# Reordering a decode kernel's loop: key transposes one quarter step ahead, VectorE's small steps one behind, values spread over four quarters, constants ahead of the query projection

## The chip, the cores and the metric

The kernel runs on one core of a Trainium2 chip. The metric is the device time of one execution, in microseconds (us). Profiled times are within the span of the core; a timed run is 1.7 to 1.8 us longer than its span (212.74 against 211.0 for the changed kernel, 224.66 against 222.9 for the profiled run of the kernel before). Each timed run comes with its granted TensorE clock and with a state: on one core, a run over 1.5% above the fastest run of the same kernel in the same set counts as slow and is left out of ratios.

## The reference, cut to what matters

One token for each of four sequences goes through an attention block and an MLP block in parallel. Attention reads a window of 2048 keys and values for 16 heads from the cache; that is nearly all of the data.

```python
# B=4, D=576, 32 query heads, 16 kv heads, 128 per head, window W=2048, F=4608
xn = _layernorm(x)
q = xn @ wq                                   # wq: 4.7 MB
scores = einsum(q, k_window) * Dh**-0.5       # k, v: 2 x 16 heads x 2 MB
o = softmax(scores) @ v_window
A = o @ wo                                    # wo: 4.7 MB
x1 = xn + gather(gelu(layernorm(xn) @ w1)) @ w2   # [the four shifts give zeros for one token]
B = x1 + gelu(layernorm(x1) @ w3) @ w4        # w3, w4: 5.3 MB each
return x + A + B
```

With one token every shifted group of `h` is padding, so the kernel never reads w1 and w2.

## The kernel before: the parts that the change touches

The loop has one step t for each head and four quarter steps s. Head t's scores, head t-1's softmax, head t-2's values and head t-3's output share a step. K arrives with positions on partitions, so VectorE transposes each quarter (`kt`) before TensorE can multiply it with the queries (`qz`). In the timelines below, the matmuls of TensorE and the instructions of VectorE each follow the order of the program, so an instruction that waits holds up those behind it. These names recur in the profiles: `kn` and `vn` are K and V tiles; `mx` is the maximum of a head's scores; `mg` is those maxima gathered by TensorE, which VectorE reduces to `nm`; `dn` is the denominator of the softmax, which VectorE inverts to `rd`; `oT` is the head's transposed output, which VectorE sums into `on`; `acc` collects the final sums.

```python
kvp = tile_pool(name="kv", bufs=6)                      # six K or V tiles of 2 MB
ktp = tile_pool(name="kt", bufs=3)
...
def k_transpose(h, s):                                  # VectorE
    kt = ktp.tile([P, 2, SC, QD], I32, tag="kt")
    nc.vector.transpose(out=kt[:], in_=src)             # quarter s of K
def k_scores(h, s):                                     # TensorE: 4 matmuls 128x512
    ...
def sm_maxT(h):
    nc.tensor.matmul(out=mg[:], lhsT=sel_jb[:], rhs=dm) # TensorE ...
    nc.vector.reduce_max(out=nm[:], in_=mg[:], ...)     # ... and VectorE at once behind it
def o_turn(h):
    ...                                                 # 4 TensorE transposes of O_sb to oT
    nc.vector.reduce_sum(out=on..., in_=oT...)          # VectorE at once behind them
# [sm_den + reciprocal, o_spread + mk and op: the same pattern]

for t in range(Hkv):
    hm, hv, hf = t - 1, t - 2, t - 3
    for s in range(NSL):
        k_transpose(t, s)
        if s == 0:
            sm_max(hm); o_turn(hf); k_mask(t)
        k_scores(t, s)
        if s == 0:   sm_maxT(hm)
        elif s == 1: sm_sub(hm); sm_exp(hm); o_spread(hf)   # o_spread, o_proj: every 4th head
        elif s == 2: o_proj(hf)
        elif s == 3: sm_turn(hm); sm_den(hm); pv(hv); o_scale(hv)
        # [t == 7: the MLP's first product and its gelu]
    # [free K tile t and V tile t-2; issue the next loads]
```

The loads go out in one order: wq, K0, K1, K2, then V(h) and K(h+3) in turn, with a wo tile ahead of V0, V4, V8 and V12, w3 between V2 and K5, and w4 last. A K or V load waits for one of the six tiles to come free.

## Time and profile before

| | kernel before |
|---|---|
| time, median of 3 (range) | 229.6 us (226.83 to 230.71) |
| span of the profiled run | 222.9 us |
| data read | 87.17 MB |
| DMA engines busy | all the time, from 5 to about 206 us |
| last scores | about 201.5 us |
| from there to the end | about 21 us |

The page of the kernel before, cut into 40 slices of 5.6 us. The digits of PE and DVE (TensorE and VectorE) are busy tenths, PEclk is the granted TensorE clock in tenths, DMA the busy share of the DMA engines:

```profile
span 222.9 us, 2388 instructions
PE   0046139759696876589763968678758756876893
DVE  4952889685667876642257568454877766374120
PEclk9999555995969999979995599958999996699589
DMA  6999999999999999999999999999999999999000
GB/s 239 429 441 435 432 421 441 425 426 429 426 420 436 444 412 435 438 435 426 429 429 426 438 426 426 435 432 432 400 405 439 438 426 429 418 431 399 16 0 2
```

The DMA row is full until slice 37, then three slices are empty while TensorE still works. Neither compute engine is full anywhere in the loop.

The costliest groups of the kernel before. After the count come busy time and mean ns, then the engine's idle time just before these instructions and what ended it:

```profile
L328 PE MATMUL S<-kt,qz 128*128 128x512 bf16 x256 | 79.6, 449 | 33.4 <-DVE kt L203 33.4
L203 DVE STREAM_TRANSPOSE kt<-kn 128x1024 int32<-128x1024 int32 x64 | 76.1, 1217 | 0.6 <-PE S L328 0.3
```

VectorE's own waits for TensorE's small results, from the list of waits (total us, times, longest):

```profile
DVE rd L365 <- PE dn L363: 23.2, 15, 4.2
DVE nm L343 <- PE mg L341: 15.5, 15, 1.1
DVE on L391 <- PE oT L385: 12.1, 14, 4.1
```

TensorE stood idle for 33.4 us waiting for transposed keys, while VectorE, which makes them, never waited for a K load (`kn`). One ordinary step of the kernel before, from the timeline (start, duration, engine, instruction, idle time before):

```profile
154.81 1.07 PE L328 MATMUL S<-kt,qz 128*128 128x512 bf16 x4
155.81 0.17 PE L341 MATMUL mg<-dm,sel_jb 128*8 128x16 bf16 x1
156.02 0.17 DVE L343 TENSOR_REDUCE nm<-mg 8x1 bf16<-8x16 f32 x1 [1.13 <-PE mg L341]
156.11 3.47 DVE L203 STREAM_TRANSPOSE kt<-kn 128x1024 int32<-128x1024 int32 x3
157.38 1.06 PE L328 MATMUL S<-kt,qz 128*128 128x512 bf16 x4 [1.40 <-DVE kt L203]
```

Here is the ping-pong: VectorE idles 1.13 us for `mg`, which stands on TensorE behind four score matmuls; the next three transposes stand on VectorE behind that wait; and TensorE then idles 1.40 us for the first of them.

The chain that ended last in the kernel before begins at 206 us, after the stream, and has no DMA in it (its longest pieces; start, duration, what):

```profile
205.97 2.25 issue
...
211.89 1.97 PE acc L307 x16
...
215.19 4.36 PE acc L307 x68
```

### The profile page before, as it was taken

To read this page: it belongs to the slowest core of one execution; us is meant where nothing else is said; L and a number is where in the kernel's file an instruction comes from. 1 tells how busy PE (TensorE), PEld (TensorE's weight loads), DVE (VectorE), ACT (ScalarE), POOL (GpSimd) and SP (SyncE) were. 2 spreads that over 40 slices of the span, in tenths; PEclk is the share of its full clock that TensorE was granted. 3 is DMA by queue.
4 is the path that set the end of the run, shared out by engine and by line. 5 is a ranking of instruction groups with operands and counts; after the bars stand their busy time and mean duration, and the time that the engine had idled before them with its cause. 6 is when DMAs were issued, how large, how long until landed. Compare 5 with 4: busy or idle time off the path is not lost. (4 is left out here: it accounts for less than half of the span.)

```text
span 222.9 us, 2388 instructions
## 1 busy us (share of the span) xinstructions
PE 148.8 (67%) x955; PEld 63.0 (28%) x955; DVE 134.1 (60%) x230; ACT 26.5 (12%) x56; POOL 13.7 (6%) x20
## 2 busy tenths in 40 slices
PE   0046139759696876589763968678758756876893
PEld 0022013222332323143331323223323321333362
DVE  4952889685667876642257568454877766374120
ACT  2001000001111211112120112101112111112110
POOL 6940030000000000000000000000000000000000
PEclk9999555995969999979995599958999996699589
DMA  6999999999999999999999999999999999999000
GB/s 239 429 441 435 432 421 441 425 426 429 426 420 436 444 412 435 438 435 426 429 429 426 438 426 426 435 432 432 400 405 439 438 426 429 418 431 399 16 0 2
DMA packets 6797, 87.32 MB, mean 392 GB/s; under 512 B 758, under 2 KB 770, under 8 KB 1282
## 3 DMA queue, kind: packets, MB, share of 16 engines
q1 hardware_dynamic: 6778, 87.17, 92.1%
q8 instruction: 7, 0.11, 0.2%
q14 instruction: 4, 0.03, 0.0%
q10 hardware_dynamic: 8, 0.00, 0.0%
HBM read 87.17 MB, written 0.00 MB: 391 GB/s over the span
## 5 line engine op out<-in xcount | busy, mean ns | idle before, releaser
L328 PE MATMUL S<-kt,qz 128*128 128x512 bf16 x256 | 79.6, 449 | 33.4 <-DVE kt L203 33.4
L203 DVE STREAM_TRANSPOSE kt<-kn 128x1024 int32<-128x1024 int32 x64 | 76.1, 1217 | 0.6 <-PE S L328 0.3
L328 PEld LDWEIGHTS <-qz 128*128 128x128 bf16 x256 | 24.7, 105 | 69.9 <-issue 56.3
L353 ACT ACTIVATE E<-S 128x512 bf16<-128x512 f32 x16 | 9.6, 597 | 97.9 <-PE S L347 97.9
L385 PE MATMUL oT<-ident_w,O_sb 128*128 128x128 f32 x64 | 11.0, 296 | 12.0 <-ACT O_sb L379 12.0
L374 PE MATMUL O<-vn,PT 128*32 128x512 bf16 x256 | 18.4, 411 | 0.0
L379 ACT ACTIVATE O_sb<-O,rd 128x512 f32<-128x512 f32 x16 | 11.0, 687 | 61.3 <-issue 43.4
L365 DVE RECIPROCAL rd<-dn 128x1 f32<-128x1 f32 x16 | 2.7, 166 | 23.2 <-PE dn L363 23.2
L359 DVE STREAM_TRANSPOSE PT<-E 128x512 bf16<-128x512 bf16 x16 | 11.2, 701 | 3.1 <-ACT E L353 3.1
L385 PEld LDWEIGHTS oT<-ident_w,O_sb 128*128 128x128 f32 x64 | 7.0, 145 | 19.7 <-ACT O_sb L379 19.5
L343 DVE TENSOR_REDUCE nm<-mg 8x1 bf16<-8x16 f32 x16 | 2.6, 164 | 15.5 <-PE mg L341 15.5
L391 DVE TENSOR_REDUCE on<-oT 128x8 bf16<-128x128 f32 x16 | 4.7, 291 | 12.1 <-PE oT L385 12.1
L334 DVE TENSOR_REDUCE mx<-S 128x1 f32<-128x512 f32 x16 | 10.5, 656 | 1.4 <-PE S L328 1.4
L188 PE MATMUL tp<-ident_bf,first 4*128 4x4 bf16 x8 | 0.6, 172 | 13.1 <-DVE first L175 13.1
L175 DVE TENSOR_SCALAR first<-first,mv,rstd 4x576 bf16<-4x576 bf16 x2 | 8.1, 4074 | 1.4 <-POOL rstd L174 1.4
L363 PEld LDWEIGHTS dn<-rs,same_j 128*128 128x128 f32 x32 | 6.7, 213 | 5.0 <-ACT E L353 1.5
L307 PE MATMUL acc<-wo_sb,op 128*32 128x288 bf16 x64 | 7.5, 405 | 0.0
L244 POOL MEMSET qz<- 128x8216 bf16 x1 | 6.9, 6934 | 0.0
L374 PEld LDWEIGHTS <-PT 128*32 128x32 bf16 x256 | 5.6, 99 | 4.6 <-issue 1.3
L347 PE MATMUL S<-nm,j_row 8*128 8x512 bf16 x16 | 6.6, 412 | 0.3 <-DVE nm L343 0.3
L319 PE MATMUL S<-negbig,ohT 4*128 4x512 bf16 x16 | 6.4, 398 | 0.0
L307 PE MATMUL acc<-w_sb,gT 128*32 128x288 bf16 x72 | 5.7, 316 | 0.0
(88 smaller groups left out, 82.5 us busy)
## 6 DMA issues: line engine op xcount, KB each, us to landing
kn<-in_A_k_cache_dram SPq DMA_DIRECT2D x16, 2048.0 KB, 18.6
vn<-in_A_v_cache_dram SPq DMA_DIRECT2D x16, 2048.0 KB, 16.0
wo_sb<-in_A_wo_dram SPq DMA_DIRECT2D x4, 1152.0 KB, 18.8
w_sb<-in_B_w_dram SPq DMA_DIRECT2D x2, 2304.0 KB, 19.1
wq_sb<-in_A_wq_dram SPq DMA_DIRECT2D x2, 2048.0 KB, 9.5
w_sb<-in_B_w_dram SPq DMA_DIRECT2D x2, 1440.0 KB, 21.3
w_sb<-in_B_w_dram SPq DMA_DIRECT2D x3, 576.0 KB, 24.7
w_sb<-in_B_w_dram SPq DMA_DIRECT2D x1, 1152.0 KB, 20.9
```

Source lines behind the costliest of these rows:

```text
L175: nc.vector.tensor_scalar(out=dst_bf[:], in0=src[:], scalar1=mv[:, 0:1], scalar2=rstd[:, 0:1], op0=ALU.subtract, op1=ALU.mult)
L203: nc.vector.transpose(out=kt[:], in_=src)
L244: nc.gpsimd.memset(qz[:], 0.0)
L307: nc.tensor.matmul(out=acc[i * QD:(i + 1) * QD, :], lhsT=lhsT, rhs=rhs[:, i * CW:(i + 1) * CW], start=False, stop=False, skip_group_check= ...
L328: nc.tensor.matmul(out=S_ps[h][:], lhsT=qz[:, z0:z0 + P], rhs=kt[:, ib, :, e:2 * QD:2].rearrange("p c k -> p (c k)"), start=False, stop=Fa ...
L334: nc.vector.reduce_max(out=mx[:], in_=S_ps[h][:], axis=AX.X)
L353: nc.scalar.activation(out=E[h][:].rearrange("p c k -> p (c k)"), in_=S_ps.pop(h)[:], func=ACT.Exp, scale=scale, accum_out=rs[:])
L359: nc.vector.transpose(out=PT[h][:], in_=E.pop(h)[:])
L363: nc.tensor.matmul(out=dn[:], lhsT=same_j[:], rhs=st.pop(("rs", h))[:], start=True, stop=True)
L374: nc.tensor.matmul(out=O_ps[h][g * QD:(g + 1) * QD], lhsT=pt[:, c, :], rhs=vn[:, :, c, :], start=(c < NQD), stop=False, skip_group_check=True)
L379: nc.scalar.activation(out=O_sb[h][:], in_=O_ps.pop(h)[:], func=ACT.Copy, scale=st.pop(("rd", h))[:, 0:1])
L385: nc.tensor.transpose(out=oT[:, s, :], in_=o[:, s, :], identity=ident_w[:, s * NJ:s * NJ + P])
```

## The change

Its intent is to keep the engines from waiting for each other inside a step: VectorE has the next transpose done before TensorE asks for it, and reads TensorE's small results a quarter or more after they were ordered. Value matmuls are cut into four groups that stand ahead of the scores. The pools `ps_s` and `ps_o` hold the scores and the value sums that TensorE writes; one buffer moves from the first to the second. In the prologue, clearing moves from GpSimd to ScalarE, and constants and the second layernorm stand ahead of the work that waits for wq.

```diff
-    ps_s bufs=3, ps_o bufs=1
+    ps_s bufs=2, ps_o bufs=2
@@ prologue
-    qz = const.tile(...); nc.gpsimd.memset(qz[:], 0.0)         # and xnT, ln2T, gT, op
+    qz = cleared([P, ZP + Hkv * 4 * P], "qz")                  # ScalarE copy of a zero
-    for kb in range(NQD):                                      # 16 small copies on VectorE
-        for ie in range(4):
-            nc.vector.tensor_copy(out=dst..., in_=qs_ps...)
+    for kb in range(NQD):                                      # 4 copies, on two engines
+        if kb % 2: nc.scalar.activation(out=dst, in_=src, func=ACT.Copy)
+        else:      nc.vector.tensor_copy(out=dst, in_=src)
     # [q_ps matmuls and all that follows them: moved behind the constants and layernorm 2]
@@ loop
+    k_transpose(0, 0)
     for t in range(Hkv):
-        hm, hv, hf = t - 1, t - 2, t - 3
+        hm, hv, hf, hp = t - 1, t - 2, t - 3, t - 4
         for s in range(NSL):
-            k_transpose(t, s)
+            if s == NSL - 1: sm_turn(hm)
+            n = t * NSL + s + 1
+            if n < Hkv * NSL:
+                k_transpose(*divmod(n, NSL))
             if s == 0:
-                sm_max(hm); o_turn(hf); k_mask(t)
-            k_scores(t, s)
-            if s == 0:   sm_maxT(hm)                           # matmul and reduce
-            elif s == 1: sm_sub(hm); sm_exp(hm); o_spread(hf)
-            elif s == 2: o_proj(hf)
-            elif s == 3: sm_turn(hm); sm_den(hm); pv(hv); o_scale(hv)
+                sm_max(hm); sm_rec(hv); o_pick(hp); o_scale(hf); k_mask(t)
+            elif s == 1: sm_maxT(hm)                           # matmul alone
+            elif s == 2: sm_sub(hm); sm_exp(hm); o_sum(hf)
+            elif s == 3: sm_den(hm)
+            pv(hv, s)                                          # 4 of 16 value matmuls
+            k_scores(t, s)
+            if s == 1:   sm_neg(hm); o_turn(hf); o_proj(hp)
+            elif s == 3: o_spread(hf)
     # [the tail is reordered in the same way; fin is one copy instead of two]
```

`sm_neg`, `sm_rec`, `o_sum` and `o_pick` are the VectorE halves of `sm_maxT`, `sm_den`, `o_turn` and `o_spread`.

More of the change, by code (lines that the diff above doesn't have):

```diff
@@ L83 @@
     small = ctx.enter_context(tc.tile_pool(name="small", bufs=2))
-    ps_s = ctx.enter_context(tc.tile_pool(name="ps_s", bufs=3, space=PSUM))
-    ps_o = ctx.enter_context(tc.tile_pool(name="ps_o", bufs=1, space=PSUM))
+    ps_s = ctx.enter_context(tc.tile_pool(name="ps_s", bufs=2, space=PSUM))
+    ps_o = ctx.enter_context(tc.tile_pool(name="ps_o", bufs=2, space=PSUM))
     ps_m = ctx.enter_context(tc.tile_pool(name="ps_m", bufs=2, space=PSUM))
@@ L155, with cleared @@
     nc.gpsimd.memset(neg_half[:], -0.5)
-    xnT = const.tile([P, KJ + 2, QD], BF16)
-    nc.gpsimd.memset(xnT[:], 0.0)
-    ln2T = const.tile([P, KJ + 2, QD], BF16)
-    nc.gpsimd.memset(ln2T[:], 0.0)
+    zero = const.tile([P, 1], I32)
+    nc.gpsimd.memset(zero[:], 0)
+    def cleared(shape, name):
+        t = const.tile(shape, BF16, name=name)
+        flat = t[:] if len(shape) == 2 else t[:].rearrange("p a b -> p (a b)")
+        flat = flat.bitcast(F32)
+        nc.scalar.activation(out=flat, in_=zero[:].bitcast(F32).to_broadcast(list(flat.shape)), func=ACT.Copy)
+        return t
+    xnT = cleared([P, KJ + 2, QD], "xnT")
+    ln2T = cleared([P, KJ + 2, QD], "ln2T")
+    ZP = (NSL - 1) * NJ
+    qz = cleared([P, ZP + Hkv * 4 * P], "qz")
+    gT = cleared([P, NF, QD], "gT")
+    op = cleared([P, WOR, QD], "op")
     RS = QD // B
@@ L204, in k_transpose @@
         kts[h, s] = kt
-    q_ps = [ps_s.tile([P, NW], F32, tag="S", name="q_ps") for _ in range(2)]
-    def q_mm(r, g, j):
-        c = r * NQD + g
-        col, k = (j * NQ + c * NW, j) if j < KJ else (KJ * NQ + g * NW, KJ + r)
-        nc.tensor.matmul(out=q_ps[r][g * QD:(g + 1) * QD, :], lhsT=xnT[:, k, :], rhs=wq_sb[:, col:col + NW],
-                         start=(j == 0), stop=False, skip_group_check=True)
-    for jr in ((0, 1), (2, 3), (KJ,)):
-        for r in range(2):
-            for j in jr:
-                for g in range(NQD):
-                    q_mm(r, g, j)
-    q_sb = bigp.tile([P, 2, NQD, Dh], BF16, tag="big", name="q_sb")
-    for r in range(2):
-        nc.scalar.activation(out=q_sb[:, r].rearrange("p u d -> p (u d)"), in_=q_ps[r][:], func=ACT.Copy)
-    qT_ps = ps_m.tile([P, 2, NQD, P], BF16, tag="m", name="qT_ps")
-    for r in range(2):
-        for u in range(NQD):
-            nc.tensor.transpose(out=qT_ps[:, r, u, :], in_=q_sb[:, r, u, :], identity=ident_bf[:])
-    q_bf = part(2 * NQD * NQD * B).rearrange("p (r g u b) -> p r g u b", r=2, g=NQD, u=NQD)
-    for r in range(2):
-        nc.vector.tensor_copy(out=q_bf[:, r],
-                              in_=qT_ps[:, r].rearrange("p u (g x) -> p g u x", g=NQD)[:, :, :, 0:B])
     sel = part(4 * P).rearrange("p (i e k x) -> p i e k x", i=2, e=2, k=NQD)
@@ L235 @@
                               in_=ident_bf[:].rearrange("p (ib i e) -> p ib e i", ib=2, e=2))
-    qs_ps = ps_m.tile([P, 4, Hkv, rep, B], F32, tag="m", name="qs_ps")
-    for ie in range(4):
-        ib, e = divmod(ie, 2)
-        nc.tensor.matmul(out=qs_ps[:, ie].rearrange("p h r b -> p (h r b)"),
-                         lhsT=sel[:, ib, e].rearrange("p k i -> p (k i)"),
-                         rhs=q_bf.rearrange("p r g u b -> p (r g u b)"), start=True, stop=True)
-    ZP = (NSL - 1) * NJ
-    qz = const.tile([P, ZP + Hkv * 4 * P], BF16)
-    nc.gpsimd.memset(qz[:], 0.0)
-    for kb in range(NQD):
-        for ie in range(4):
-            dst = qz[kb * QD:(kb + 1) * QD, ZP:].rearrange("p (h i m) -> p h i m", h=Hkv, i=4)
-            nc.vector.tensor_copy(out=dst[:, :, ie, kb * QD:kb * QD + NJ].rearrange("p h (b r) -> p h b r", r=rep),
-                                  in_=qs_ps[kb * QD:(kb + 1) * QD, ie].rearrange("p h r b -> p h b r"))
     oh4 = const.tile([P, B], F32)
@@ L282 @@
     sel_wo = const.tile([P, WOR, WOH, WOD], BF16)
-    nc.gpsimd.tensor_copy(out=sel_wo[:], in_=ident_bf[:].rearrange("p (d i) -> p i d", i=WOR).unsqueeze(2)
-                          .to_broadcast([P, WOR, WOH, WOD]))
+    nc.scalar.activation(out=sel_wo[:], in_=ident_bf[:].rearrange("p (d i) -> p i d", i=WOR).unsqueeze(2)
+                         .to_broadcast([P, WOR, WOH, WOD]), func=ACT.Copy)
     own = const.tile([P, WOH], F32)
@@ L298, with q_mm @@
     transposed(ln2_bf, ln2T)
-    gT = const.tile([P, NF, QD], BF16)
-    nc.gpsimd.memset(gT[:], 0.0)
-    op = const.tile([P, WOR, QD], BF16)
-    nc.gpsimd.memset(op[:], 0.0)
+    q_ps = [ps_s.tile([P, NW], F32, tag="S", name="q_ps") for _ in range(2)]
+    def q_mm(r, g, j):
+        c = r * NQD + g
+        col, k = (j * NQ + c * NW, j) if j < KJ else (KJ * NQ + g * NW, KJ + r)
+        nc.tensor.matmul(out=q_ps[r][g * QD:(g + 1) * QD, :], lhsT=xnT[:, k, :], rhs=wq_sb[:, col:col + NW],
+                         start=(j == 0), stop=False, skip_group_check=True)
+    for jr in ((0, 1), (2, 3), (KJ,)):
+        for r in range(2):
+            for j in jr:
+                for g in range(NQD):
+                    q_mm(r, g, j)
+    q_sb = bigp.tile([P, 2, NQD, Dh], BF16, tag="big", name="q_sb")
+    for r in range(2):
+        nc.scalar.activation(out=q_sb[:, r].rearrange("p u d -> p (u d)"), in_=q_ps[r][:], func=ACT.Copy)
+    qT_ps = ps_m.tile([P, 2, NQD, P], BF16, tag="m", name="qT_ps")
+    for r in range(2):
+        for u in range(NQD):
+            nc.tensor.transpose(out=qT_ps[:, r, u, :], in_=q_sb[:, r, u, :], identity=ident_bf[:])
+    q_bf = part(2 * NQD * NQD * B).rearrange("p (r g u b) -> p r g u b", r=2, g=NQD, u=NQD)
+    for r in range(2):
+        nc.vector.tensor_copy(out=q_bf[:, r],
+                              in_=qT_ps[:, r].rearrange("p u (g x) -> p g u x", g=NQD)[:, :, :, 0:B])
+    qs_ps = ps_m.tile([P, Hkv, 4, rep, B], F32, tag="m", name="qs_ps")
+    for ie in range(4):
+        ib, e = divmod(ie, 2)
+        nc.tensor.matmul(out=qs_ps[:, :, ie], lhsT=sel[:, ib, e].rearrange("p k i -> p (k i)"),
+                         rhs=q_bf.rearrange("p r g u b -> p (r g u b)"), start=True, stop=True)
+    for kb in range(NQD):
+        rows = slice(kb * QD, (kb + 1) * QD)
+        dst = qz[rows, ZP:].rearrange("p (x m) -> p x m", m=P)[:, :, kb * QD:kb * QD + NJ].rearrange("p x (b r) -> p x b r", r=rep)
+        src = qs_ps[rows].rearrange("p h i r b -> p (h i) b r")
+        if kb % 2:
+            nc.scalar.activation(out=dst, in_=src, func=ACT.Copy)
+        else:
+            nc.vector.tensor_copy(out=dst, in_=src)
     def acc_matmuls(lhsT, rhs):
@@ L341, in sm_maxT, with sm_neg @@
         nc.tensor.matmul(out=mg[:], lhsT=sel_jb[:], rhs=st.pop(("dm", h))[:], start=True, stop=True)
+        st["mg", h] = mg
+    def sm_neg(h):
         nm = small.tile([NJ, 1], BF16, tag="nm")
-        nc.vector.reduce_max(out=nm[:], in_=mg[:], axis=AX.X, negate=True)
+        nc.vector.reduce_max(out=nm[:], in_=st.pop(("mg", h))[:], axis=AX.X, negate=True)
         st["nm", h] = nm
@@ L363, in sm_den, with sm_rec, pv @@
         nc.tensor.matmul(out=dn[:], lhsT=same_j[:], rhs=st.pop(("rs", h))[:], start=True, stop=True)
-        rd = small.tile([P, 1], F32, tag="rd", bufs=3)
-        nc.vector.reciprocal(out=rd[:], in_=dn[:])
+        st["dn", h] = dn
+    def sm_rec(h):
+        rd = small.tile([P, 1], F32, tag="rd", bufs=4)
+        nc.vector.reciprocal(out=rd[:], in_=st.pop(("dn", h))[:])
         st["rd", h] = rd
-    def pv(h):
-        O_ps[h] = ps_o.tile([P, NSL, Dh], F32, tag="O", name="O")
+    def pv(h, s):
+        if s == 0:
+            O_ps[h] = ps_o.tile([P, NSL, Dh], F32, tag="O", name="O")
         vn = kv_tiles["V", h][:].rearrange("p (s c) d -> p s c d", s=NSL)
-        pt = PT.pop(h)
-        for c in range(SC):
-            g = c % NQD
-            nc.tensor.matmul(out=O_ps[h][g * QD:(g + 1) * QD], lhsT=pt[:, c, :], rhs=vn[:, :, c, :],
-                             start=(c < NQD), stop=False, skip_group_check=True)
+        for g in range(NQD):
+            c = s * NQD + g
+            nc.tensor.matmul(out=O_ps[h][g * QD:(g + 1) * QD], lhsT=PT[h][:, c, :], rhs=vn[:, :, c, :],
+                             start=(s == 0), stop=False, skip_group_check=True)
+        if s == NSL - 1:
+            PT.pop(h)
     def o_scale(h):
@@ L385, in o_turn, with o_sum @@
             nc.tensor.transpose(out=oT[:, s, :], in_=o[:, s, :], identity=ident_w[:, s * NJ:s * NJ + P])
+        st["oT", h] = oT
+    def o_sum(h):
+        oT = st.pop(("oT", h))
         v = oT[:].rearrange("p s (g x) -> p (s g) x", g=NQD)[:, :, 0:NJ].rearrange("p g (b r) -> p b r g", r=rep)
@@ L402, in o_spread, with o_pick @@
                              rhs=on[:].rearrange("p h b -> p (h b)"), start=True, stop=True)
+        st["R"] = R
+    def o_pick(h):
+        if h % WOQ < WOQ - 1:
+            return
+        R = st.pop("R")
         mk = small.tile([P, WOR, WOH, B], BF16, tag="mk")
@@ L486 @@
     G_AT = 7
+    k_transpose(0, 0)
     for t in range(Hkv):
-        hm, hv, hf = t - 1, t - 2, t - 3
+        hm, hv, hf, hp = t - 1, t - 2, t - 3, t - 4
         for s in range(NSL):
-            k_transpose(t, s)
+            if s == NSL - 1 and hm >= 0:
+                sm_turn(hm)
+            n = t * NSL + s + 1
+            if n < Hkv * NSL:
+                k_transpose(*divmod(n, NSL))
             if s == 0:
@@ L493 @@
                     sm_max(hm)
+                if hv >= 0:
+                    sm_rec(hv)
+                if hp >= 0:
+                    o_pick(hp)
                 if hf >= 0:
-                    o_turn(hf)
+                    o_scale(hf)
                 k_mask(t)
-            k_scores(t, s)
-            if s == 0 and hm >= 0:
+            elif s == 1 and hm >= 0:
                 sm_maxT(hm)
-            elif s == 1:
+            elif s == 2:
                 if hm >= 0:
@@ L504 @@
                 if hf >= 0:
-                    o_spread(hf)
-            elif s == 2:
-                if hf >= 0:
-                    o_proj(hf)
-            elif s == 3:
-                if hm >= 0:
-                    sm_turn(hm)
-                    sm_den(hm)
-                if hv >= 0:
-                    pv(hv)
-                    o_scale(hv)
+                    o_sum(hf)
+            elif s == 3 and hm >= 0:
+                sm_den(hm)
+            if hv >= 0:
+                pv(hv, s)
+            k_scores(t, s)
+            if s == 1:
+                if hm >= 0:
+                    sm_neg(hm)
+                if hf >= 0:
+                    o_turn(hf)
+                if hp >= 0:
+                    o_proj(hp)
+            elif s == 3 and hf >= 0:
+                o_spread(hf)
             if t == G_AT:
@@ L529 @@
     sm_max(hl)
-    o_turn(hl - 2)
+    sm_rec(hl - 1)
+    o_scale(hl - 2)
+    pv(hl - 1, 0)
     sm_maxT(hl)
+    sm_neg(hl)
+    pv(hl - 1, 1)
     sm_sub(hl)
     sm_exp(hl)
+    o_turn(hl - 2)
+    pv(hl - 1, 2)
+    pv(hl - 1, 3)
+    o_sum(hl - 2)
     sm_turn(hl)
     sm_den(hl)
-    pv(hl - 1)
+    sm_rec(hl)
     o_scale(hl - 1)
+    for s in range(NSL):
+        pv(hl, s)
+    o_scale(hl)
     o_turn(hl - 1)
-    pv(hl)
-    o_scale(hl)
+    o_sum(hl - 1)
     pieces = list(zip(W4_PIECES, W4_PIECES[1:]))
@@ L543 @@
     o_turn(hl)
+    o_sum(hl)
     o_spread(hl)
+    o_pick(hl)
     mlp_out(*pieces[1])
@@ L550 @@
     fin = const.tile([2 * QD, CW], out.dtype)
-    nc.vector.tensor_copy(out=fin[:, 0:CW // 2], in_=acc[0:2 * QD, 0:CW // 2])
-    nc.scalar.activation(out=fin[:, CW // 2:CW], in_=acc[0:2 * QD, CW // 2:CW], func=ACT.Copy)
+    nc.vector.tensor_copy(out=fin[:], in_=acc[0:2 * QD, :])
     nc.sync.dma_start(out=o2.rearrange("b (i n) -> i b n", i=2), in_=fin[0:2 * QD:RS, :])
```

## The prediction

> **What bounds it now.** The span is 222.9 us. The table of stretches shows a DMA share of 0.99 to 1.04 in every stretch from 5 to 205 us, at 418 to 442 GB/s: the kernel streams 87.2 MB and the queue is never empty. That agrees with the Trainium skill, "DMA: Bandwidth & Descriptors", section "Where 436 GB/s comes from" (ceiling 435). After about 206 us the DMA is idle, and 16.9 us of compute follow. So time = stream (to about 206) + tail (16.9).
>
> The tail exists because compute runs late. The timeline shows the first key transpose on VectorE at 32.6 us, the last scores at about 201.5. After K15's load come only V13, V14, V15 and w4 (11.6 MB, 27 us at 429 GB/s), so it should have landed near 179: compute trails by about 16 us. VectorE never waits for a K load; the loop is a ping-pong: TensorE waits 33.4 us for kt, VectorE 23.2 for dn, 15.5 for mg, 12.1 for oT (list of waits). A step takes 169/16 = 10.5 us, against 4.19 MB / 429 GB/s = 9.8 us of DMA.
>
> **What the change does.**
> - Prologue. The first layernorm's multiply took 7.0 us on VectorE (the second 1.1), ending with GpSimd's 6.9 us clearing of qz. The Trainium skill, "SBUF — State Buffer", "Who interferes with whom", says such VectorE operations and GpSimd lock each other out of a shared port; the durations agree. Clearing moves to ScalarE (about 3 us, estimated from 0.32 us for 144 and 0.60 for 512 columns), constants and second layernorm (25.3 to 32.7 us) go under the wq load, 16 qz copies (3.6 us) become 4 on two engines. First key transpose: about 20 us, when K0 lands, not 32.6.
> - Loop. No work is removed: VectorE per step stays 4x1.22 + 0.70 + 0.66 + 0.23 + 0.29 + 0.17 + 0.16 = 7.1 us, TensorE about 8. The waits for kt, mg, dn and oT mostly vanish, so compute per step can drop below 9.8 us and follow the loads. Waits for V and K landings appear; buffers are reissued earlier, so loads in flight rise.
> - The stream gains nothing: it still ends at about 205 to 206.
>
> **On the critical path.** Only the tail. If V14 and V15 (about 189 and 194) are used soon after landing, what follows the last w4 piece is 8 matmuls (about 1 us), fin (about 0.45) and the output DMA (2.7 from issue to the end): about 4.3 us. I allow 2 us for pv15, turns and acc matmuls not yet done. Span 206 + 4.3 + 2 = 212, i.e. -11 us. The timed median of before (229.6) is 6.7 above its profiled span, presumably partly lateness at a lower clock; with slack I expect less of that: about 215 us (range 210 to 221.5). Chances: faster by over 2% 0.94, within 2% 0.05, slower 0.01.
>
> **What would show it.** First key transpose near 20 us; first-layernorm multiply near 1 us; idle of scores on kt well below 10 us; new TensorE waits on V landings and VectorE waits on K landings; median K landing above 22 us (was 18.6); DMA share still 1.0, ending at 205 to 206; last scores near 193; tail of 5 to 9 us, w4's DMA on the chain or just off it.
>
> **What would make it wrong.** TensorE at a low clock: four half-clock score matmuls take 1.81 us against 1.07, and waits on loads may keep the clock low, so the last steps trail and the tail stays near 12. VectorE blocked in order behind a key transpose whose K has not landed. Two S buffers, not three, coupling steps. A slower stream in timed runs, which no reordering can mend.

## The result, and the profile after

| | before | after |
|---|---|---|
| time, median (range) | 229.83 us (226.83 to 230.71), 4 runs | 212.74 us (212.73 to 212.80), 4 runs |
| ratio of fast runs (95%) | 1 | 0.930 (0.921 to 0.939) |
| span of the profiled run | 222.9 us | 211.0 us |

A ratio is the mean time of one kernel's fast runs over the mean of the other's fast runs of the same rounds, so it is not quite the ratio of the medians. In this small set the runs of the kernel before that count as fast are 226.83, 229.60 and 230.06 us; two of them would count as slow beside the later runs, so 0.930 flatters the change. The outcome is a clear gain, and well inside the predicted range.

The size depends on how the kernel before happens to run. Over the 27 runs of it that accompanied the later experiments it took 223.89 to 226.80 us in nine fast runs, at a granted clock of 0.862 or 0.863, and 228.09 to 231.64 us in the others, at 0.828 to 0.849. The mean of the nine is 225.07 us, against which 212.75 us (mean of the four runs after) is 5.5% less; this compares fast runs with fast runs and is the figure to keep. The changed kernel's time did not follow its clock: 0.858 to 0.868 in its four runs, all within 0.07 us.

The page of the changed kernel, same rows but the last (slices of 5.3 us):

```profile
span 211.0 us, 2402 instructions
PE   0386695869395009669999499968693967898982
DVE  4832989485731082825725968985867284763220
PEclk9999579799859655957999669999998596969998
DMA  7999999999999999999999999999999999999990
```

The DMA row is now full to the last slice but one. The same groups, and the value matmuls:

```profile
L335 PE MATMUL S<-kt,qz 128*128 128x512 bf16 x256 | 82.0, 452 | 3.1 <-DVE kt L215 3.1
L215 DVE STREAM_TRANSPOSE kt<-kn 128x1024 int32<-128x1024 int32 x64 | 76.8, 1221 | 10.3 <-DMA kn<-in_A_k_cache_dram 9.4
L387 PE MATMUL O<-vn,PT 128*32 128x512 bf16 x256 | 27.8, 434 | 38.5 <-DMA vn<-in_A_v_cache_dram 36.9
```

The work is the same (82.0 us of scores, 76.8 us of transposes), but the wait for `kt` fell from 33.4 to 3.1 us, and TensorE now waits 36.9 us for V and VectorE 9.4 us for K. TensorE now waits for data and hardly for VectorE. VectorE's waits for two of TensorE's small results did not shrink, though. In the list of waits of the changed kernel (total us, times, longest):

```profile
DVE nm L353 <- PE mg L348: 20.2, 10, 3.8
DVE on L410 <- PE oT L400: 15.7, 13, 1.8
```

They were 15.5 and 12.1 us before; what they are now is settled by a run without loads, below, and by this piece of the changed kernel's timeline:

```profile
162.86 0.62 PE L387 MATMUL O<-vn,PT 128*32 128x512 bf16 x4 [3.40 <-DMA vn<-in_A_v_cache_dram]
163.41 1.89 PE L335 MATMUL S<-kt,qz 128*128 128x512 bf16 x4
165.22 0.18 PE L348 MATMUL mg<-dm,sel_jb 128*8 128x16 bf16 x1
165.44 0.16 DVE L353 TENSOR_REDUCE nm<-mg 8x1 bf16<-8x16 f32 x1 [3.10 <-PE mg L348]
```

TensorE waited for V until 162.86 us and had four value and four score matmuls to do before `mg`, the latter at low clock (1.89 us against 1.08 in the step below). VectorE had run out of work at 162.34 and so waited 3.10 us. An ordinary step of the changed kernel, from the timeline:

```profile
134.80 1.23 DVE L215 STREAM_TRANSPOSE kt<-kn 128x1024 int32<-128x1024 int32 x1
134.87 0.17 PE L348 MATMUL mg<-dm,sel_jb 128*8 128x16 bf16 x1
134.88 0.40 PE L387 MATMUL O<-vn,PT 128*32 128x512 bf16 x4
135.21 1.08 PE L335 MATMUL S<-kt,qz 128*128 128x512 bf16 x4
135.95 0.12 DVE L353 TENSOR_REDUCE nm<-mg 8x1 bf16<-8x16 f32 x1
136.00 1.22 DVE L215 STREAM_TRANSPOSE kt<-kn 128x1024 int32<-128x1024 int32 x1
```

`mg` is ordered at 134.87 and read at 135.95, behind a transpose that VectorE had in hand; neither line shows an idle time. The end of the chain that ended last in the changed kernel:

```profile
155.73 24.30 DMA kn<-in_A_k_cache_dram
180.05 26.94 DMA w_sb<-in_B_w_dram
207.03 0.68 PE acc L314 x8
207.73 0.45 DVE fin L601
```

The last w4 piece lands at 207.0 us; eight matmuls and one copy follow, and the output's DMA takes the rest. Before, 16.9 us followed the stream; now 4.0 us do.

One more view is worth making by hand, since no page shows it: the times at which the maximum of each head's scores starts on VectorE (`mx`), from the timelines. They mark the steps.

| kernel | first key transpose | `mx` of head 4 | `mx` of head 15 | between (11 steps) | from there to the end |
|---|---|---|---|---|---|
| before | 32.6 | 76.7 | 202.0 | 125.3 | 20.9 |
| after | 21.7 | 76.5 | 194.0 | 117.4 | 17.0 |

The changed kernel starts its first transpose 10.9 us earlier, and yet both reach head 4 at the same time. So the gain of 11.9 us in the span comes from the later steps (about 7.9) and what follows the last `mx` (3.9), and the earlier start is worth nothing by then. The reordered tail was not tested by itself: TensorE had 14.3 us of work behind the last `mx` before and 11.2 after, at a mean clock of 0.84 and 0.97, and which of the tail's edits matters is not shown. The step times of the kernel before also show that its mean of 10.5 us per step hid a mixture: between heads 4 and 15 steps without extra work took 7.6 to 9.1 us (one, behind the MLP, 10.6), the three with an output projection 13.9, 14.9 and 14.8, and the one with the MLP 19.7.

### The profile page after: what moved, and what is told of

Its sections match the earlier page's. It is cut to its first block, busy times and chain, and to the rows that moved or that the text cites. A ratio compares the mean times of both kernels' runs of the same rounds, so it can differ in the third digit from the quotient of the medians.

```text
span 211.0 us, 2402 instructions
## 1 busy us (share of the span) xinstructions
PE 150.4 (71%) x955; PEld 62.2 (29%) x955; DVE 121.3 (57%) x216; ACT 33.9 (16%) x63; POOL 2.8 (1%) x15
## 4 chain that ended last, share of the span: by engine, by line
DMA 67%; PE 18%; DVE 7%; issue 4%; ACT 1%; SPq 1%; POOL 0%; POOLq 0%; DVEq 0%
DMA w_sb<-in_B_w_dram 29%; DMA vn<-in_A_v_cache_dram 26%; DMA kn<-in_A_k_cache_dram 12%; PE S L335 9%; DVE kt L215 3%; PE g_ps L453 2%; PE q_ps L277 2%; PE O L387 2%; PE oT L400 1%; PE acc L314 1%; DMA first<-in_A_x_dram 1%; DVE qz L309 1%; PE gT_ps L465 1%; DVE mx L341 1%; PE S L357 1%
## 5 line engine op out<-in xcount | busy, mean ns | idle before, releaser
L335 PE MATMUL S<-kt,qz 128*128 128x512 bf16 x256 | 82.0, 452 | 3.1 <-DVE kt L215 3.1
L215 DVE STREAM_TRANSPOSE kt<-kn 128x1024 int32<-128x1024 int32 x64 | 76.8, 1221 | 10.3 <-DMA kn<-in_A_k_cache_dram 9.4
L387 PE MATMUL O<-vn,PT 128*32 128x512 bf16 x256 | 27.8, 434 | 38.5 <-DMA vn<-in_A_v_cache_dram 36.9
L335 PEld LDWEIGHTS <-qz 128*128 128x128 bf16 x256 | 22.2, 106 | 43.2 <-issue 28.5
L387 PEld LDWEIGHTS <-PT 128*32 128x32 bf16 x256 | 7.3, 95 | 47.2 <-DVE kt L215 23.8
L369 DVE STREAM_TRANSPOSE PT<-E 128x512 bf16<-128x512 bf16 x16 | 11.4, 711 | 14.3 <-ACT E L363 14.3
L353 DVE TENSOR_REDUCE nm<-mg 8x1 bf16<-8x16 f32 x16 | 2.5, 154 | 20.3 <-PE mg L348 20.2
L410 DVE TENSOR_REDUCE on<-oT 128x8 bf16<-128x128 f32 x16 | 4.6, 286 | 15.7 <-PE oT L400 15.7
L341 DVE TENSOR_REDUCE mx<-S 128x1 f32<-128x512 f32 x16 | 10.5, 658 | 1.3 <-PE S L335 1.3
L400 PEld LDWEIGHTS oT<-ident_w,O_sb 128*128 128x128 f32 x64 | 9.6, 167 | 5.4 <-issue 3.9
L348 PE MATMUL mg<-dm,sel_jb 128*8 128x16 bf16 x16 | 2.8, 175 | 3.7 <-DVE dm L343 3.7
L348 PEld LDWEIGHTS <-sel_jb 128*8 128x8 bf16 x16 | 1.3, 83 | 12.6 <-issue 6.7
L453 PE MATMUL g_ps<-w_sb,ln2T 128*32 128x512 bf16 (+1 forms) x50 | 4.9, 443 | 0.0
L314 PE MATMUL acc<-wo_sb,op 128*32 128x288 bf16 x64 | 4.6, 287 | 0.0
L373 PE MATMUL dn<-rs,same_j 128*128 128x1 f32 x32 | 4.6, 212 | 0.0
## 6 DMA issues: line engine op xcount, KB each, us to landing
kn<-in_A_k_cache_dram SPq DMA_DIRECT2D x16, 2048.0 KB, 22.3
```

The lines of the kernel that those rows point to most:

```text
L314: nc.tensor.matmul(out=acc[i * QD:(i + 1) * QD, :], lhsT=lhsT, rhs=rhs[:, i * CW:(i + 1) * CW], start=False, stop=False, skip_group_check= ...
L335: nc.tensor.matmul(out=S_ps[h][:], lhsT=qz[:, z0:z0 + P], rhs=kt[:, ib, :, e:2 * QD:2].rearrange("p c k -> p (c k)"), start=False, stop=Fa ...
L341: nc.vector.reduce_max(out=mx[:], in_=S_ps[h][:], axis=AX.X)
L369: nc.vector.transpose(out=PT[h][:], in_=E.pop(h)[:])
L373: nc.tensor.matmul(out=dn[:], lhsT=same_j[:], rhs=st.pop(("rs", h))[:], start=True, stop=True)
L387: nc.tensor.matmul(out=O_ps[h][g * QD:(g + 1) * QD], lhsT=PT[h][:, c, :], rhs=vn[:, :, c, :], start=(s == 0), stop=False, skip_group_check ...
```

## The experiments

Twelve kernels were run. Theory A says that the kernel before was bound by its own engine-to-engine waits, late behind a stream that ran at full speed anyway, and that the changed kernel is bound by the stream. The rivals are named with each run. Kernels of which only a part of the data is loaded compute something else on purpose; the comparison with the reference nevertheless passed for all twelve, so its tolerance does not see an attention output made from the wrong tiles, and a pass says little about these terms.

### The two halves of the change, each alone

`p_only` has the new prologue with the old loop and tail, `l_only` the old prologue with the new loop and tail.

```diff
# p_only: kernel before, with
+ everything of the change up to the queries in qz      # pools, loop and tail as before
# l_only: changed kernel, with
- everything of the change up to the queries in qz      # pools, loop and tail as changed
```

> The new prologue (constants, clearing and second layernorm ahead of wq) with the old loop and tail. Theory A (the gain is the removal of lateness: what counts is whether compute has caught up with the loads by the end; either part may do most of it alone): the first key transpose moves to about 21.7 us, the old loop then waits for the w3 load and ends its last scores at 194 to 196 (201.5 before), the tail behind them is the old 21 us, so 214 to 218 us. Rival B (the two parts add, the prologue being the smaller): 222 us or more. DMA share 1.0 to about 206 either way.

> The old prologue with the new loop and tail. Theory A: compute starts at 32.6 us as before, catches up with the loads while they bring w3 (by about 80 us), and from there it is the changed kernel: 212.7 to 213.5 us, TensorE waiting for V landings in the second half. Rival B (parts add): 217 us or more.

Measured: `p_only` 226.38 us median (224.38 to 226.77), ratio 1.005 (0.995 to 1.016) to the kernel before: no gain. `l_only` 212.72 us (212.71 to 212.79), ratio 0.946 (0.942 to 0.950): the whole gain, since the complete change takes 212.73 to 212.80. The first expectation missed by about 10 us, and its time lies where rival B put it (222 us or more), though not for the rival's reason: the two halves add up only because the first is worth nothing. The second held.

The profile of `p_only` says where its head start went. Its DMA stream brings w3 (5.3 MB) between V2 and K5, and no attention step uses w3. From its timeline:

```profile
41.37 0.55 SPq L102 DMA_DIRECT2D kn<-in_A_k_cache_dram  x1
74.29 1.25 DVE L215 STREAM_TRANSPOSE kt<-kn 128x1024 int32<-128x1024 int32 x1 [12.65 <-DMA kn<-in_A_k_cache_dram]
75.46 0.65 DVE L341 TENSOR_REDUCE mx<-S 128x1 f32<-128x512 f32 x1
75.59 1.86 PE L335 MATMUL S<-kt,qz 128*128 128x512 bf16 x4 [11.30 <-DVE kt L215]
```

K5 was issued at 41.37 us, behind w3, and VectorE stood idle for 12.65 us until it landed. The kernel before reached K5 at 75.55 us, after the 74.29 at which `p_only` could go on, and did not wait; `l_only`, which starts as late but has the faster loop, had already caught up and waited 10.2 us for it. Head 4's `mx` is at 75.5 us in `p_only`, 76.7 in the kernel before, 76.5 in the changed one and 76.7 in `l_only`. From there the old loop took 128.4 us to head 15 in `p_only` (mean clock of TensorE 0.84) and 125.3 in the kernel before (0.89); the new loop took 117.4, and 115.6 in `l_only`. The mistake in the expectation was to let the old loop trail the loads only slightly once it had caught up with them. Its mean step after w3 is 11.7 us in `p_only` (128.4 / 11), against 9.8 us for a pair of K and V loads, so it fell behind again.

### Is the stream the bound? Fewer bytes

Three of the four wo loads (3.54 MB) are left out; the first tile is used four times.

```diff
     def load_wo(p):
+        if p > 0:
+            wo_tiles[p] = wo_tiles[0]
+            return
         t = wop.tile([P, WOR, D], BF16, tag="wo", name="wo_sb")
```

> The changed kernel with three of the four wo loads left out (one tile used four times; the output is wrong on purpose): 3.54 MB or 8.2 us less of the stream at 429 GB/s. Theory A (the changed kernel is bound by the stream): about 8 us less, 204.5 to 206 us. Rival C (compute of the last steps binds as well): under 3 us less.

> The kernel before with the same three wo loads left out. Theory A (its compute is late and sets the end; the busy DMA does not): at most 2 us less than the kernel before. Rival D (it is bound by the stream as well, and only its tail is longer): about 8 us less.

Measured: the changed kernel took 204.95 us (204.92 to 205.03), 7.8 us less; the kernel before took 225.16 and 226.58 us in its fast runs, ratio 1.005 (0.989 to 1.020), nothing less. The rate of the DMA in `b_wo1` (its profiled run is a slow one, so only the pattern is read here) shows that the queue now runs dry in places, at no gain:

```profile
GB/s 249 441 418 432 421 450 425 412 444 439 425 424 439 421 435 432 424 438 430 421 297 412 280 401 357 432 297 352 340 405 417 435 421 430 417 426 198 3 0 1
```

So a full DMA row did not make the kernel before bound by the stream. The likely reason that it was full, which no run tests: six tiles of prefetch let the loads run ahead of a late loop, and the loop's pace happened to be nearly that of the loads.

### The loop's own pace, without loads

Only the first three K and V tiles are loaded and used for all heads. No later step waits for a load, so the step times are those of the engines.

```diff
     def load_kv(kind, h):
+        if h >= 3:
+            kv_tiles[kind, h] = kv_tiles[kind, h % 3]
+            return
```

> The kernel before with only the first three K and V tiles loaded and used again for all heads (output wrong on purpose), so that no step waits for a load: the loop's own pace. Theory A: 10 to 10.5 us per step, as with all loads, since that loop never waited for a K load; span 215 to 223 us. Rival (its loop is paced by freed buffers and loads): under 9.5 us per step.

> The changed kernel with the same three K and V tiles used for all heads. Theory A: 8 to 9 us per step without waits on VectorE and TensorE for each other, last scores at about 21.7 + 16 x 8.5 = 158 us, span 170 to 178 us. Rival (the reordering only moved waits): 10 us per step, span over 195 us.

Measured: the kernel before took 224.81 us in its one fast run (230.16 to 231.58 in three slow ones), as much as with all its loads (223.93 and 226.80 in the fast runs of the same rounds). The changed kernel took 163.76 to 165.19 us in its fast runs. The span of that fast run, 223.0 us, is at the edge of the expected 215 to 223; the mean step of the profiled, slow run, from its `mx` times, was 11.3 us, above the expected 10 to 10.5. So 54.5 MB less of data changed nothing for the old loop, as far as one fast run can say; it takes about 60 us more than the new one when both are free of loads (224.81 less 164.64, the mean of three). The old loop's whole time was its own, and the new loop has about 48 us in hand (212.75 less 164.64), of which the stream now takes all. The changed kernel's estimate was even too cautious (170 to 178 us): undisturbed steps took 6.8 us rather than 8 to 9. The windows of the profile of `a_res` for one stretch of two such steps show why they can hardly be shorter:

```profile
core 0: us, PE busy (x) PEld busy (x) DVE busy (x) ACT busy (x) POOL busy (x), PEclk, DMA share, GB/s
128.50:142.20 13.70, 13.23 (x91) 5.63 (x90) 12.72 (x22) 2.75 (x6) 0.00 (x0) 1.00 0.44 185
```

TensorE is busy for 13.23 and VectorE for 12.72 of 13.70 us, at full clock. In the kernel before, two undisturbed steps (153.3 to 170.8 us) took 17.5 us at the same full clock, with 12.98 us of TensorE work.

The list of waits of the same run answers for `mg` and `oT`:

```profile
DVE on L413 <- PE oT L403: 5.3, 4, 1.6
DVE nm L356 <- PE mg L351: 3.3, 2, 3.1
```

Without loads the two waits are 3.3 and 5.3 us. The 20.2 and 15.7 us under the full stream are therefore mostly the wait for V, handed on, with the low clock that goes with it: `mg` and `oT` stand on TensorE behind value matmuls that wait for a landing, as in the piece at 162.86 us above. In `b_res` (profiled in a slow run), by contrast, the wait for `kt` is 33.4 and that for `mg` 15.5 us, exactly as with all loads.

### Which part of the reordering does it

All four kernels below are the changed kernel; the first three have the resident tiles as well, so that the stream does not hide the effect. `a_res_nok` has the transposes back in their own quarter step, `a_res_nd` the small VectorE steps straight behind the TensorE work, `a_res_both` both, and `a_res_nopv` all value matmuls in the last quarter.

```diff
# a_res_nok                                # a_res_nd
-    k_transpose(0, 0)                     -  elif s == 1: sm_maxT(hm)
-    k_transpose(*divmod(n, NSL))          +  after k_scores, s == 0: sm_maxT(hm); sm_neg(hm)
+    k_transpose(t, s)                     +  o_sum, sm_rec, o_pick straight behind
# a_res_nopv                               +    o_turn, sm_den, o_spread
-    pv(hv, s)
+    if s == NSL - 1: pv(hv, 0) ... pv(hv, 3)
```

> As the changed kernel with the resident tiles, but key transposes in the same quarter step as the scores that read them. If running them ahead is what hides the transposes: 1.0 us or more per step slower than with them ahead. If the deferral of the small steps and the values in between hide them already: under 0.5 us per step.

> As the changed kernel with the resident tiles, but VectorE's small steps (nm, on, rd, mk and op) straight behind the TensorE work that they read, the transposes still one ahead. If the small steps stall VectorE in order and so delay transposes that TensorE needs: 0.5 to 1.5 us per step slower. If the one step of lead of the transposes covers that: under 0.3 us per step.

> The changed loop with resident tiles, both the lead of the key transposes and the delay of the small steps undone, the values still spread. The single undoings cost 18.8 and 6.0 us. If the two are separate: about 190 us. If each hides what the other leaves (a stalled VectorE matters most when no transpose is in hand, and the stalls let TensorE's clock fall): 200 us or more, towards the 225 to 231 us of the loop before.

> The changed loop with resident tiles, all 16 value matmuls of a head in the last quarter step. If the spread only matters where something has to cover a wait, and the lead of the transposes has left none: within 3 us of 165 us. If it is what keeps TensorE busy between the quarter steps: 10 us or more slower.

| resident tiles | fast runs, us | mean over `a_res` | undisturbed step |
|---|---|---|---|
| `a_res` (as changed) | 163.76 to 165.19 | | 6.8 |
| `a_res_nok` | 182.67 to 185.15 | +19.2 | 7.9 |
| `a_res_nd` | 170.86 to 172.41 | +6.7 | 7.1 |
| `a_res_both` | 203.88 to 206.78 | +41.3 | 9.0 |
| `a_res_nopv` | 156.58 to 158.12 | -7.1 | 6.6 |
| `b_res` (as before) | 224.81 | +60.2 | 8.7 |

The step is the commonest one at full clock in the profiled run; those of `a_res` and `b_res` fell on slow runs, so there only such undisturbed steps are read.

The lead of the transposes is the larger part and the delay of the small steps the smaller, but the two undone together cost 41.3 us, more than their sum (25.9). The undisturbed steps, all at full clock, show the same (1.1, 0.3 and 2.2 us more), so the lower clock of `a_res_both` (0.908 in its profile) is not the whole reason. For `a_res_nd` neither expectation held: 6.7 us are 0.4 us per step, between the two. Each hides what the other leaves: with a transpose in hand, a stalled VectorE delays nothing that TensorE needs at once. A step of `a_res_both`, from its timeline, shows the same knot as the kernel before:

```profile
159.16 0.17 DVE L356 TENSOR_REDUCE nm<-mg 8x1 bf16<-8x16 f32 x1 [0.80 <-PE mg L351]
159.25 1.22 DVE L218 STREAM_TRANSPOSE kt<-kn 128x1024 int32<-128x1024 int32 x1
160.53 1.07 PE L338 MATMUL S<-kt,qz 128*128 128x512 bf16 x4 [1.17 <-DVE kt L218]
```

The spread of the value matmuls was expected to help or to be neutral, and it costs: 7.1 us without loads. Part of it is measured per step, 6.8 against 6.6 us. Four groups of four take 0.33 us each from start to start of what follows (121.00 to 121.33 in the timeline of `a_res`), 1.32 us in all, while one group of 16 takes 0.98 (117.60 to 118.58 in that of `a_res_nopv`). Of these 0.34 us a head, 0.2 show in the step, some 3 us over the heads. In `a_res` TensorE also waited 3.9 us for the first V tile to land, ahead of head 2's scores, and that step took 11.6 us; in `a_res_nopv` it did not wait, and the step took 6.2. The profile of `a_res` fell on a slow run, but `a_res_nd`, spread as well and profiled in a fast run, has the same wait (3.5 us) and the same long step (10.4 us against its ordinary 7.1). So most of the remaining 4 us or so is probably this one early wait. With all loads the spread's cost would be hidden; the spread was not undone there, so whether it does any good in the full kernel stays open. Nor were the 18.9 us between `a_res_both` and `b_res` taken apart; the later start (33.2 against 21.8 us in the profiles), the buffers and the tail are in them.

### Does a slower loop matter under the stream?

`a_nok` is the changed kernel with all its loads and with the transposes back in their own quarter step.

> The changed kernel with all its loads, key transposes back in the quarter step of their scores. With resident tiles this cost 1.2 us per step (182.67 to 185.15 us against 163.76 to 166.27), 7.9 us per ordinary step. Theory A (the stream's pace of 9.8 us is all that counts once the loop is faster than it): 212.7 to 213.5 us, no loss. Rival (the wait adds to the wait for loads, as TensorE takes both in order): 216 us or more.

Measured: 212.83 us (212.70 to 212.85), the same as the complete change. A loop that is 19 us slower by itself costs nothing here, because 183.9 us of compute still fit under the stream. One wait took the place of another: TensorE's matmuls waited 21.3 us for `kt` and 23.5 us for V, where they had waited 3.1 and 36.9.

```profile
PE O L387 <- DMA vn<-in_A_v_cache_dram: 23.5, 7, 13.1
PE S L335 <- DVE kt L215: 21.3, 18, 3.1
```

So with all loads the lead of the transposes was not needed to reach the stream: the rest of the new loop and tail was enough. Whether the lead alone would be enough was not run.

### A version that beats both

`a_end` has the last w4 piece cut from four rows of chunks to two, so that four matmuls instead of eight follow the last landing.

```diff
-    W4_PIECES = [0, 10, NFH, NFH + 10, NFH + 14, NF]
+    W4_PIECES = [0, 10, NFH, NFH + 10, NFH + 16, NF]
```

> The changed kernel with the last w4 piece cut from 4 to 2 rows of chunks, so that 4 instead of 8 matmuls follow the last landing. Theory A: the span ends 0.3 us sooner, 212.3 to 212.5 us. If smaller packets slow the last loads: no gain, or 0.2 us slower.

Measured: 212.47 us median (212.38 to 212.57, six runs), and the six lie below all four runs of the changed kernel (212.73 to 212.80). They were not timed in the same rounds, so the 0.27 us rests on how little both vary. `a_nok`, which was timed in the same rounds and ends like the changed kernel, took 212.70 to 212.85. The 0.27 us is the size that was expected, but the trace differs from the reckoning: TensorE resumed at 206.29 us on the piece before the last and ran 16 matmuls (1.16 us) without waiting for the last one, which landed at about 206.9 (issued at 180.0, 26.9 to landing). The end of the stream is hidden behind matmuls there, and little is left other than bytes.

## Why the prediction was right, point by point

- **Bound and mechanism: right.** The predicted sum was a stream to about 206 us and a tail that shrinks from 16.9 to about 6 us, for a span of 212. Measured were a stream to 207.0 and 4.0 us behind it, a span of 211.0. The allowance of 2 us for matmuls left over at the end was not needed; the stream itself ended 1 us later than predicted.
- **The loop: right in its result, wrong about two waits.** The wait of scores on `kt` fell to 3.1 us ("well below 10"), new waits on V (36.9) and K (9.4) appeared, the last scores began at 193.6 ("near 193"), and the median time of a K load from issue to landing rose from 18.6 to 22.3 us ("above 22"), as tiles were freed and reissued earlier. VectorE's wait for `dn` (23.2) left the list. But "the waits for kt, mg, dn and oT mostly vanish" failed for `mg` and `oT`, which rose to 20.2 and 15.7 us: they vanish only without loads (3.3 and 5.3), and under the stream they hand on the wait for V. `a_wo1` shows the new bound directly, `b_res` the old one.
- **The prologue: its times were right, its weight was not.** The first transpose came at 21.7 us ("about 20"). The text counted this start as a part of the lateness that makes the tail ("The tail exists because compute runs late. The timeline shows the first key transpose on VectorE at 32.6 us"). `p_only` and `l_only` show that it has no part in it: the w3 load makes early and late starters meet at head 4. The total was right without it because neither half of the account could do more than reach the stream; in this the number was helped by that limit and not by the reasoning.
- **The pace of the old loop.** "A step takes 169/16 = 10.5 us" is a mean over steps of 7.5 to 19.7 us. That it hardly exceeded 9.8 us made the lateness look as if it came largely from the start; from head 4 on the mean was 11.4 us (125.3 / 11), and that is what made the tail.
- **The first layernorm's multiply: right in kind.** It fell from 7.0 us to 0.44 (predicted near 1). The Trainium skill, "SBUF — State Buffer", section "Who interferes with whom", states that such a VectorE operation and GpSimd can exclude each other for a whole instruction. The traces agree: before, the multiply ended at 11.39 us and the clearing at 11.22. In `l_only`, where GpSimd clears `qz` again, it takes 7.02 us again. The second multiply, 1.13 us before beside a smaller clearing, takes 0.41 us after.
- **What was predicted for timed runs: mis-sized by 1.3 us.** The prediction added 3 us to the span of 212, for the difference between a timed run and its profiled span; measured were 1.7 us, the plain difference, without lateness at a low clock. With the span 1 us shorter than predicted, this makes the 2.3 us between 215 and 212.74. The risk named, a low clock, did occur in the loop (PEclk is down to 5 in some slices) and cost nothing, as the loop has time in hand. The kernel before has none, and its slow runs are those at the lower clock (0.828 to 0.849 against 0.862 and 0.863); which of the two causes the other is not shown.

## What to carry to other kernels

A full DMA row says that the queue is never empty, not that the time hangs on it: take bytes away, or take the loads away altogether, and see whether the time moves. When a loop is a ping-pong between two in-order engines, move the producer one step ahead and the reader of small results one step behind: with the tiles resident, undoing both cost more than the sum of undoing each. Then compare the loop's own pace with the stream's to know when to stop; under the stream the first of the two could be left out here at no cost. Work moved earlier in the prologue is worth something only if nothing downstream makes early and late starters meet.

## What the Trainium skill lacked or had wrong

- "DMA: Bandwidth & Descriptors", section "Where 436 GB/s comes from", gives 435 GB/s as the ceiling of the ports but says that for transfers between HBM and SBUF the HBM side binds at about 358, without saying when. The condition stands in another section, "Measured (HBM→SBUF, 128 partitions, SWDGE, issued from GpSimd)": 425 for a core whose neighbour is idle, and about 358 for each when both stream. This one-core kernel read HBM at 418 to 442 GB/s in every stretch from 5 to 205 us; the ceiling of the ports is the figure that fits. Whether the neighbouring core was idle is not shown by these runs.
- "Perfetto Trace Analysis", section "What 'DMA-bound' means", lists the resources that can bind but not the test. The kernel before had a DMA share of 0.99 to 1.04 throughout, and took 224.81 us with 54.5 MB of its loads left out against 223.93 and 226.80 with them. Prefetch that keeps a queue full hides that the loop is the slower one.
- "TensorE: Matmul & The Clock Gate", section "What's actually happening", states that the clock is set by how busy TensorE has lately been. The traces agree in kind: four score matmuls take 1.06 to 1.08 us at full clock and up to 1.89 at low clock, and the mean clock in the profiles is higher where TensorE is busier (0.86 at 67% busy in the kernel before, 0.967 at 85% in `a_res_nopv`). The page says that the number of slow matmuls at the start varies from run to run, but not that the same kernel can fall into runs of 223.9 to 226.8 us and of 228.1 to 231.6 us, at granted clocks of 0.862 and of 0.828 to 0.849, while a kernel bound by its stream stays within 0.07 us.
- "TensorE: Matmul & The Clock Gate", Part 3, describes tiles that overlap within one pack. It gives no cost for breaking a run of packs: four packs of four tiles took 0.33 us each between other matmuls and 0.98 us for all four in a row.
